# A hand-written step order for linear attention feeding a multiplicative FFN: the steps after chunk 1's first gate tile in another sequence

## The chip, the cores and the metric

The kernel runs on one core of a Trainium2 chip. The metric is the device time of one execution in microseconds (us). The kernel before takes 247.02 us as the median of three runs, which lie between 246.37 and 248.18 us.

## The reference

Eight batches of eight heads, 576 positions and 64 features per head go through a linear attention, and its output, as 4608 tokens of 512 features, goes through a feed-forward block with a product in its middle:

```
phi(x) = max(x, 0) + 1 where x > 0, exp(x) otherwise          # elu + 1
kv  = einsum('bhsd,bhde->..', phi(k), v);  z = sum_s phi(k)   # per batch and head: 64 x 64, and 64
x   = (phi(q) @ kv) / (phi(q) @ z + 1e-6)                     # 4608 tokens x 512
out = ((x @ w1) * (x @ w2)) @ w3 @ w_out                      # 512 -> 1024 -> 1024 -> 512
```

## The kernel before

**Chunks.** A batch is a chunk of 512 tokens; the 64 left over of every batch are gathered into a ninth chunk, number 8. Weights, phi, the attention products and the FFN are in bf16 with f32 sums. At the start, w3 and w_out are multiplied into one 1024 x 512 matrix wf_sb (steps E, C, w, u). Then each chunk runs through the stages below, and the stages of several chunks overlap.

**Steps.** The whole program is one string, ORDER, that `step` (L644) reads word by word. Every word issues a few instructions, each on its own engine, and every engine runs what it was given strictly in that order. So ORDER sets five queues at once: those of the TensorE (PE), VectorE (DVE), ScalarE (ACT), GpSimd (POOL) and SyncE (SP). A trailing `+` is the variable alt: a copy goes to DVE and not to ACT, a load goes on POOL's queue and not on SP's, and in step A the `+1e-6` goes to ACT and not to DVE. With b the chunk:

- L, M, N b.g load half g of k, q, v (512 KB each, L112) into one of 13 buffers of the pool `ld`; R b.0 loads the tails of q and k (four DMAs of 64 KB, L122), R b.1 those of v.
- x, X (exp on ACT, L187), y, Y (max and add on DVE, L192) and z, Z (min on DVE, L216) make phi of k and of q; part 2 is the tail. v b.i casts v (L222, tail L228).
- T b transposes phi(q) by a DMA from SP (L276). K b makes kv on PE (L252) and copies it out of PSUM (L261).
- A b.j makes 128 normalised tokens: four matmuls (L317), then an add (L334 on DVE or L332 on ACT), a reciprocal and a product on DVE (L335, L336). j = 4 is the tail. D b transposes the result into the tile xt by a DMA from SP (L361); for chunks 0 and 1 step P does it on PE (L351, L352).
- F c.f and the pair h, i are one tile of (x @ w1) * (x @ w2) for chunks 0 to 2: eight matmuls of 512 columns into two PSUM banks (L372), a copy on ACT (L377), a product on DVE (L378).
- G c.q.i is the same for chunks 3 to 8 in a Strassen-like form with seven products instead of eight: four matmuls of 256 columns (L435), then one of L464, L467, L473 on ACT, L470 and L474 on DVE; m is the closing product (L479). d c.i makes the differences of xt (L420) and e w.i those of the weights (L409) that it needs.
- O c.m multiplies by wf_sb (eight matmuls of 512 columns, L550) and copies out (L552); S and H store. Q is the last of these.

**PSUM and other limits.** F, G and the last O take four PSUM banks (`mm_ps`), G's accumulators and O two banks (`o_ps`), K and A share one double bank (`at_ps`, `bufs=1`), so A waits for the product of the A before it. Chunk c's F or G tiles need the whole tile xt, so the first of them waits for the landing of D c. SP keeps eight DMAs in flight at most: each new one waits for the eighth before it.

**Gates.** `GATES` makes two loads wait for another step's DMA (R6.0 for T3.0, M2.1 for B0.0).

Of the kernel before, what the change touches and what calls it, by code (L numbers as in the profile page):

```python
# [20 lines left out]
def kernel(  # L21
# [570 lines left out]
    E4 E3 C0 E1 E0 I0 M0.0 C1 I1+ C2 I2+ W0.8 w4 W1.5 w3+ R0.1 v0.2 Y0.0 u4.0 u3.0 C3 w1+ R0.0 E5
    w0+ E6 L0.1+ E2 u1.0 u0.0 E7 M0.1+ u4.1 u3.1 L0.0+ u0.1 x0.2 u0.2 u3.2 y0.2 u1.1 u1.2 z0.2 u3.3+
    u4.2 u4.3 u1.3 w5+ w6 N0.1 N0.0+ u0.3+ u5.0 u5.1 u6.0 u6.1 X0.0 y0.1 Z0.0 M1.1+ u6.2 x0.1 u6.3+
    z0.1 w2 Y0.1 X0.1 w7 M1.0+ R1.0+ B3.0 L1.0+ Z0.1 u5.2 y0.0 u5.3 u2.0 u2.1 x0.0 u2.2 u2.3+ B3.1
    a0.0+ z0.0 u7.0 u7.1 a0.1+ X1.1 Y1.1 u7.2 K0 N1.1 L1.1+ X1.0 I3 Z1.1 a0.2 R1.1+ Y1.0 u7.3 A0.2
    a1.1 A0.3 W2.4 A0.0 P0.2 A0.1 Z1.0 x1.2 x1.0 y1.0 P0.3 W3.2 A0.4 y1.2 N1.0 P0.0 W4.2 P0.1 y1.1
    B2.0 x1.1 v1.2 z1.2 B2.1 a1.0 z1.0 B1.0 z1.1 F0.7 F0.6 K1+ F0.4 a1.2 A1.2 F0.5 B0.0 I4 P1.2 A1.1
    B1.1 F0.2 B0.1 P1.1 M2.1 M3.1 A1.3 F0.3 P1.3 X2.1 R2.0+ A1.0 L2.1 h0 h1 Y2.1 P1.0 M2.0 h2 h3
    Z2.1 i0 i1 X3.1 R3.0+ A1.4 x2.1 F1.7 F1.6 x2.2 y2.2 Y2.0 M3.0 z2.2 e1.0 R2.1 x3.2 X2.0 Z2.0 N2.0  # L600
    y2.1 z2.1 L2.0 O0.0 Y3.0 X3.0 N2.1 R3.1 F1.0 T2.0 v2.0+ F1.3 L3.0 v2.2 L3.1 R4.0 Z3.0 O0.2 Y3.1
    x2.0 y2.0 z2.0 e1.1 y3.2 z3.2 N3.1 v2.1 F1.2 O0.1+ N3.0 S0.0 e0.2 K2 F1.5 A2.2 Z3.1 x3.0 F1.4
    A2.1+ F1.1 x3.1 A2.0+ y3.0 O0.3 T3.0 S0.1 y3.1 A2.3+ D2.0 z3.0 z3.1 v3.2 v3.0 v3.1 O1.2+ O1.3
    R4.1 e1.3 R6.0+ M4.0 M4.1 e0.0 e0.1 e0.3 K3 O1.0 A3.1+ O1.1 L4.0 A3.2+ e1.2 F2.1 A3.0+ N4.1 F2.5
    A3.3+ D3.0 Y4.0 L4.1 v4.2 F2.7 S1.1 N4.0 Y4.1 y4.2 X4.1 Z4.1 F2.2 A2.4+ x4.2 X4.0 F2.0 v4.1 z4.2
    Z4.0 T4.0 F2.3 M5.1 d3.2 L5.0 M5.0 S1.0 y6.2 L5.1 d3.0 R5.0+ F2.4 y5.2 d3.1 x6.2 x4.0 y4.0 z4.0
    G3.1.1 F2.6 A3.4+ v4.0+ y4.1 G3.1.3 x4.1 z4.1 G3.1.2 x5.2 O2.2 G3.1.4 z5.2 d3.3 G3.1.5 m3.1.5
    G3.0.4 G3.0.1 K4 z6.2 G3.0.3 G3.1.6 G3.1.7 A4.2+ G3.0.5 N5.0 y5.0 R5.1+ v5.2 m3.0.5 G3.0.2 Y5.1
    X5.1 O2.3 S2.1 G3.0.7 x5.0 Z5.1 G3.0.6 z5.0 Y5.0 A4.0+ X5.0 Z5.0 O2.1 m3.0.6 x5.1 O2.0 y5.1 L6.0
    N5.1 L6.1 G3.3.1 G3.3.4 S2.0 T5.0 A4.1+ z5.1 G3.2.1 m3.1.6 G3.3.3 G3.2.4 G3.2.3 G3.3.5 G3.3.2  # L610
    v5.0 G3.2.5 A4.3+ D4.0 G3.3.7 G3.2.2 v5.1 G3.3.6 G3.2.7 G3.2.6 m3.2.5 m3.2.6 x6.1 O3.1 x6.0 K5
    m3.3.5 M6.1 D1.1 m3.3.6 O3.3 y6.0 z6.0 y6.1 A5.2 z6.1 O3.2 d4.0 d4.1 d4.2 A5.0+ d4.3 G4.1.1
    G4.1.4 R6.1 X6.1 Y6.1 Z6.1 D3.1 O3.0 A5.1+ G4.1.3 G4.1.6 G4.0.1 G4.1.5 v6.2 G4.0.4 A5.3 G4.0.3
    G4.1.7 G4.0.2 G4.0.5 N6.0 v6.0 m4.1.5 G4.1.2 G4.3.1 G4.0.6 G4.0.7 A4.4+ G4.3.3 N7.1 G4.3.4 M6.0
    Y6.0 G4.2.1 G4.3.5 D5.0 d5.0 G4.3.6 X6.0 Z6.0 N6.1 G4.2.3 G4.2.2 G4.2.4 S3.1 G4.3.7 G4.2.5
    G5.0.4 v6.1 d5.1 m4.1.6 G4.2.6 G5.1.1 G4.2.7 m4.3.6 d5.2 K6 m4.3.5 L7.0 m4.0.5 G5.0.1 m4.2.5
    G5.1.2 L7.1 d5.3 G5.1.3 m4.0.6 G5.0.3 G5.0.6 G5.1.4 G5.0.5 G5.0.2 G5.1.5 G5.0.7 m4.2.6 G4.3.2
    T6.0 A6.3+ G5.1.7 y7.1 S3.0 x7.0 x7.1 O4.2 A6.0 R7.0 O4.1 y7.0 G5.2.1 z7.0 A6.2 z7.1 G5.1.6
    G5.3.1 N7.0 G5.3.4 G5.2.3 A6.1 G5.3.3 G5.2.2 G5.2.4 G5.3.5 x7.2 G5.2.5 G5.3.2 M7.1 G5.3.7 X7.1
    M7.0 G5.2.6 m5.0.6 G5.2.7 Y7.0 m5.2.5 R7.1 v7.2 m5.1.6 m5.1.5 m5.3.5 D6.0 d6.2 d6.0 Y7.1 A5.4+  # L620
    O4.3 S4.1 d6.1 m5.2.6 v7.1 O4.0 Z7.1 X7.0 Z7.0 y7.2 z7.2 G6.1.1 v7.0 G6.1.4 G5.3.6 O5.0 G6.1.3
    G6.3.4 T7.0 S4.0 m5.0.5 G6.1.6 d6.3 G6.0.1 D5.1 G6.1.2 A6.4+ m5.3.6 G6.1.5 G6.0.3 G6.0.4 G6.2.4
    G6.0.5 K7+ G6.1.7 G6.0.7 m6.1.6 G6.0.2 A7.1 G6.3.1 O5.2 G6.3.3 G6.0.6 G6.2.1 G6.3.5 G6.3.2 A7.4
    G6.2.3 G6.3.7 m6.0.6 G6.2.2 G6.2.6 G6.2.5 m6.2.5 O5.1 D7.1 m6.1.5 d8.0 G6.3.6 G6.2.7 d8.1 m6.3.6
    S5.0 A7.3+ O5.3 G8.0.1 G8.0.4 G8.1.1 d8.2 A7.0 G8.0.3 G8.0.6 G8.1.3 d8.3 G8.0.5 G8.1.4 G8.1.5
    S5.1 G8.2.4 G8.0.7 G8.0.2 G8.1.7 G8.1.2 m6.2.6 G8.2.1 G8.1.6 m6.0.5 G8.3.1 m6.3.5 G8.2.3 G8.2.6
    G8.3.3 m8.1.5 G8.2.5 G8.3.4 G8.3.5 G8.3.2 G8.2.7 A7.2+ G8.2.2 G8.3.7 D7.0 d7.0 m8.0.6 O6.2 O6.1
    O6.0 S6.0 O6.3 G7.0.1 d7.1 d7.3 d7.2 G8.3.6 m8.3.6 G7.1.1 S6.1 G7.0.3 G7.0.4 m8.3.5 G7.1.3
    G7.0.5 m7.0.5 G7.1.4 G7.1.5 G7.0.6 G7.0.7 G7.0.2 G7.1.7 G7.1.6 G7.2.1 G7.1.2 m8.0.5 G7.3.1
# [121 lines left out]
```

## Time and profile before

| | us |
|---|---|
| median of three runs | 247.02 (246.37 to 248.18) |
| span of the profiled execution, first to last instruction | 245.6 |
| the profiled execution's own time | not recorded beside its span; the runs are 0.8 to 2.6 above the span |
| PE busy | 230.7 |
| DVE busy | 189.6 |
| ACT busy | 158.9 |
| POOL busy | 37.8 |

The granted TensorE clock is 0.999 in this execution, so nothing is lost there. The busy time of PE contains overlaps of matmuls that follow each other: a 512-column matmul is shown with 379 ns, and eight of them in a row take 1.73 us of the chain of waits, 0.216 us each. DVE instructions overlap too: a product that is shown with 0.69 us holds its engine for 0.60 us. The 16 DMA engines are busy in nine tenths or more of the time until two thirds of the span, then little.

### The profile page before, as it was taken

The numbers are of one execution on the slowest core, as the hardware profiler recorded it, in microseconds if no ns is written. First come the engines' busy times: TensorE is split into PE (matmuls) and PEld (weight loads), VectorE is DVE, ScalarE is ACT, GpSimd is POOL, SyncE is SP. The second block draws the span as 40 slices with busy tenths as digits, with TensorE's granted clock in tenths as the row PEclk, the third lists the DMA queues.
The fourth block names the chain that finished last, engine by engine and source line by source line (L and its number), as shares of the span: only waits on it lengthen the run. The fifth ranks groups of instructions, "written<-read, shape, count | busy, mean of one in ns | idle before, by whom it ended". The sixth has DMA issues, their size and how long they took to land.

```text
span 245.6 us, 4685 instructions
## 1 busy us (share of the span) xinstructions
PE 230.7 (94%) x1713; PEld 146.7 (60%) x1713; DVE 189.6 (77%) x416; ACT 158.9 (65%) x296; POOL 37.8 (15%) x61
## 2 busy tenths in 40 slices
...
DMA  7999999999999999999999999987281320440065
GB/s 147 195 202 299 297 244 216 192 236 312 295 185 303 287 198 270 190 335 291 353 324 180 229 245 263 269 242 164 85 157 49 103 93 0 88 171 3 0 191 151
DMA packets 68343, 49.46 MB, mean 201 GB/s; under 512 B 37088, under 2 KB 63456, under 8 KB 68320
## 3 DMA queue, kind: packets, MB, share of 16 engines
...
## 4 chain that ended last, share of the span: by engine, by line
PE 69%; DMA 12%; DVE 10%; ACT 5%; issue 2%; POOL 0%; DVEq 0%; ACTq 0%; POOLq 0%
PE o_ps L550 19%; PE gu L435 15%; PE gt L435 11%; PE a_ps L372 9%; PE b_ps L372 8%; DMA w3b<-in_moe_w_dram 7%; DMA q<-in_q_dram 5%; PE nd L317 3%; DVE y L192 2%; DVE spare L470 2%; PE kvp L252 1%; DVE xn L336 1%; ACT e L187 1%; DVE kj L216 1%; DVE ab L474 1%
## 5 line engine op out<-in xcount | busy, mean ns | idle before, releaser
L550 PE MATMUL o_ps<-wf_sb,ab 128*128 128x512 bf16 x280 | 64.2, 379 | 0.0
L550 PEld LDWEIGHTS <-ab 128*128 128x128 bf16 x280 | 26.9, 98 | 29.1 <-DVE ab L474 0.8
L552 ACT COPY o_sb<-o_ps 128x512 f32<-128x512 f32 x31 | 18.1, 584 | 26.1 <-PE o_ps L550 24.9
L435 PEld LDWEIGHTS <-w_sb 128*128 128x128 bf16 x288 | 28.0, 98 | 6.8 <-issue 2.0
L372 PEld LDWEIGHTS <-w_sb 128*128 128x128 bf16 x192 | 18.2, 98 | 19.4
L372 PE MATMUL b_ps<-xt,w_sb 128*128 128x512 bf16 x96 | 25.6, 379 | 0.0
L372 PE MATMUL a_ps<-xt,w_sb 128*128 128x512 bf16 x96 | 25.6, 379 | 0.0
L336 DVE TENSOR_TENSOR xn<-nd,r 128x512 bf16<-128x512 f32 x30 | 20.7, 691 | 2.1
L378 DVE TENSOR_TENSOR ab<-a_sb,b_ps 128x512 bf16<-128x512 f32 x24 | 16.1, 683 | 6.5 <-ACT a_sb L377 3.9
L187 ACT ACTIVATE e<-q 128x1024 bf16<-128x1024 f32 x16 | 17.0, 1060 | 5.8 <-DMA q<-in_q_dram 5.7
L435 PEld LDWEIGHTS <-wt_sb 128*128 128x128 bf16 x192 | 18.2, 98 | 4.1 <-issue 0.3
L435 PEld LDWEIGHTS <-spare 128*128 128x128 bf16 x192 | 18.7, 98 | 2.2
L187 ACT ACTIVATE e<-k 128x1024 bf16<-128x1024 f32 x16 | 16.9, 1061 | 3.8 <-DMA k<-in_k_dram 3.8
L479 DVE TENSOR_TENSOR ab<-spare 128x256 bf16<-128x256 f32 x48 | 18.5, 417 | 0.1
L435 PE MATMUL gu<-spare,wt_sb 128*128 128x256 bf16 x96 | 18.3, 272 | 0.2
L435 PE MATMUL gu<-spare 128*128 128x256 bf16 x96 | 18.3, 272 | 0.0
L470 DVE TENSOR_TENSOR spare<-spare,gt 128x512 f32<-128x512 f32 x24 | 16.2, 680 | 2.2 <-PE gt L435 2.2
L470 DVE TENSOR_TENSOR spare<-spare,gu 128x512 f32<-128x512 f32 x24 | 16.2, 680 | 2.0 <-PE gu L435 1.9
L162 PE MATMUL wf_ps<-wt_sb,w3t 128*128 128x512 bf16 x64 | 15.3, 379 | 2.5 <-DMA wt_sb<-in_moe_w_out_dram 1.1
L317 PE MATMUL nd<-kv,qt 128*128 128x130 bf16 (+1 forms) x160 | 15.8, 220 | 1.5 <-ACT kv L261 1.3
L377 ACT COPY a_sb<-a_ps 128x512 f32<-128x512 f32 x24 | 13.6, 585 | 5.3 <-PE a_ps L372 5.1
L317 PEld LDWEIGHTS <-qt 128*128 128x128 bf16 (+1 forms) x160 | 11.2, 99 | 8.8 <-issue 3.3
...
## 6 DMA issues: line engine op xcount, KB each, us to landing
...
```

Source lines behind the costliest of these rows:

```text
L162: nc.tensor.matmul(wfs[i], w3ts[i][:, kc, :], wo_sb[:, kc, :], start=(kc == 0), stop=(kc == FC - 1))
L187: nc.scalar.activation(out=e, in_=x, func=AF.Exp)
L317: nc.tensor.matmul(nds[g][rows, i * 2 * E1:(i + 1) * 2 * E1], w, kvs[b % 2][:, i, g].rearrange("p u e -> p (u e)"), start=True, stop=True)
L336: nc.vector.tensor_tensor(out=dst.rearrange("p (g h) e -> p g h e", g=2), in0=v4[:, :, :, 0:D], in1=r[rows].unsqueeze(3).to_broadcast([n, ...
L372: nc.tensor.matmul(ps, w[:, kc, f * P:(f + 1) * P], xt_of(c)[:, :, kc, :], start=(kc == 0), stop=(kc == KC - 1))
L377: nc.scalar.copy(out=a_sb, in_=a_ps)
L378: nc.vector.tensor_mul(out=abs_[c][:, f, :], in0=a_sb, in1=b_ps)
L435: nc.tensor.matmul(t[:, w], l, r, start=(first and w == 0 and k == 0), stop=(k == 1), skip_group_check=True)
L470: nc.vector.tensor_tensor(out=s, in0=s, in1=t, op=ALU.add)
L479: (nc.gpsimd if alt else nc.vector).tensor_mul(out=abs_[c][:, f, r * HN:(r + 1) * HN], in0=s[:, 0], in1=s[:, 1])
L550: nc.tensor.matmul(o_ps, ab[:, f, m * P:(m + 1) * P], wf_sb[:, f, :], start=(f == 0), stop=(f == FC - 1))
L552: copy_of(alt)(out=rows_of(c, m // 2)[:, m % 2], in_=o_ps)
```

## The change

Up to step L2.1 the order is the same word for word; there the program has come to step h0, the first of the last two gate tiles of chunk 0, and PE to 54.85 us of the profile. The 530 steps that follow are the same steps in another sequence. In 34 of them the `+` is put on or taken off. No instruction is added or taken away, no shape changes, and GATES stays as it is. (The W steps only lose a number that nothing reads.)

```
     ORDER = """
...
-    B1.1 F0.2 B0.1 P1.1 M2.1 M3.1 A1.3 F0.3 P1.3 X2.1 R2.0+ A1.0 L2.1 h0 h1 Y2.1 P1.0 M2.0 h2 h3
-    Z2.1 i0 i1 X3.1 R3.0+ A1.4 x2.1 F1.7 F1.6 x2.2 y2.2 Y2.0 M3.0 z2.2 e1.0 R2.1 x3.2 X2.0 Z2.0 N2.0
...
+    P1.2 A1.1 B1.1 F0.2 B0.1 P1.1 M2.1 M3.1 A1.3 F0.3 P1.3 X2.1 R2.0+ A1.0 L2.1 N2.1 Y2.1 Z2.1 R3.0
+    h0 L3.0 x2.2 h1 M2.0 h2 P1.0+ M3.0 h3 e1.0 e1.1 i0 i1 Y3.1 y2.1 A1.4+ X3.1 N2.0 e0.2 F1.2 O0.0
...
     """
     GATES = "R6.0<T3.0 M2.1<B0.0"
```

The 34 changes of engine or queue:

- ACT to DVE: the copies of P1.0, O1.0, O1.1, O5.2, O5.3, O6.0, O6.1, O8.1, O8.2, v2.1, v2.2, v5.2, v6.2, v7.2 and K6, and the add of A2.0, A2.4, A3.0, A3.1, A4.2, A4.3 and A6.3.
- DVE to ACT: the copies of O0.1, O7.2 and v2.0, and the add of A1.4, A6.0, A6.2 and A7.4.
- POOL to SP: the tail loads R3.0, R5.0, R5.1 and R6.0. SP to POOL: the load N6.1.

**SP, around the transpose of chunk 2** (`xt<-xn` is D2.0 and then D3.0, `qt<-qj` is T3.0, `qk32r` and `v32r` are tails, q, k, v the 512 KB loads). Before:

```order
L276 DMA_TRANSPOSE qt<-qj 128x18x128
L560 DMA out_dram<-o_sb 128x1024
L361 DMA_TRANSPOSE xt<-xn 128x16x128
L122 DMA v32r<-in_v_dram 64x4x64 x2
L112 DMA q_1173<-in_q_dram 128x4x256
L112 DMA q_1175<-in_q_dram 128x4x256
L112 DMA k_1232<-in_k_dram 128x4x256
L112 DMA v_1267<-in_v_dram 128x4x256
L361 DMA_TRANSPOSE xt<-xn 128x16x128
```

Now:

```order
L276 DMA_TRANSPOSE qt<-qj 128x18x128
L560 DMA out_dram<-o_sb 128x1024
L361 DMA_TRANSPOSE xt<-xn 128x16x128
L112 DMA k_1191<-in_k_dram 128x4x256
L112 DMA q_1193<-in_q_dram 128x4x256
L112 DMA k_1228<-in_k_dram 128x4x256
L122 DMA qk32r<-in_q_dram 64x4x64 x2
L122 DMA qk32r<-in_k_dram 64x4x64 x2
L112 DMA v_1237<-in_v_dram 128x4x256
L112 DMA q_1241<-in_q_dram 128x4x256
L361 DMA_TRANSPOSE xt<-xn 128x16x128
```

Between the transposes of chunks 2 and 3 SP issued a tail of v and four big loads; now it issues five big loads and the four tail loads R5.0, which stood on POOL's queue.

**DVE, around the differences of chunk 3** (`spare<-xt` at L420 are the steps d3, which read the xt that D3.0 brings; L378 closes an F tile). Before:

```order
L212 TENSOR_TENSOR qj<-er,yr 128x512
L216 TENSOR_TENSOR qj<-e,y 128x4x256
L378 TENSOR_TENSOR ab<-a_sb,b_ps 128x512
L420 TENSOR_TENSOR spare<-xt 128x512
L192 TENSOR_SCALAR yr<-qk32r 128x512
L420 TENSOR_TENSOR spare<-xt 128x512
L378 TENSOR_TENSOR ab<-a_sb,b_ps 128x512
L192 TENSOR_SCALAR yr<-qk32r 128x512
L420 TENSOR_TENSOR spare<-xt,spare 128x512
```

Now:

```order
L378 TENSOR_TENSOR ab<-a_sb,b_ps 128x512
L192 TENSOR_SCALAR y<-q_1241 128x1024
L216 TENSOR_TENSOR kj<-e,y 128x4x256
L420 TENSOR_TENSOR spare<-xt 128x512
L378 TENSOR_TENSOR ab<-a_sb,b_ps 128x512
L420 TENSOR_TENSOR spare<-xt,spare 128x512
L216 TENSOR_TENSOR qj<-e,y 128x4x256
L378 TENSOR_TENSOR ab<-a_sb,b_ps 128x512
```

The first d3 stood behind the products of all F tiles but two; one F tile more is now behind it.

**ACT, around the load L5.1** (`e<-k` are x5.0 and x5.1; L552 copies O2.x out, L464 and L467 serve the first G tiles). Before:

```order
L187 ACTIVATE e<-k_1385 128x1024
L332 ACTIVATE r<-nd,eps 128x8
L187 ACTIVATE e<-q_1387 128x1024
L552 COPY o_sb<-o_ps 128x512
L187 ACTIVATE e<-k_1392 128x1024
L552 COPY o_sb<-o_ps 128x512
L464 COPY gt<-gu 128x512
L467 COPY spare<-gt_1674 128x512
L332 ACTIVATE r<-nd,eps 128x8
L464 COPY gt<-gu 128x512
```

Now:

```order
L187 ACTIVATE e<-k_1499 128x1024
L332 ACTIVATE r<-nd,eps 128x8
L187 ACTIVATE e<-k_1617 128x1024
L552 COPY o_sb<-o_ps 128x512 x2
L464 COPY gt<-gu 128x512 x2
L467 COPY spare<-gu 128x512
L332 ACTIVATE r<-nd,eps 128x8
L467 COPY spare<-gu 128x512
L467 COPY spare<-gt_1712 128x512
```

The exp of the last k half of chunk 5 stood between the copies of two O tiles, and now stands ahead of both.

More of the change, by code (lines that the diff above doesn't have):

```diff
@@ L591 @@
     ORDER = """
[L592 to L629, printed above, removed]
@@ L630 @@
-    m8.1.6 G7.2.3 G7.2.4 G7.3.3 m8.2.6 G7.3.4 G7.2.5 G7.2.2 G7.3.2 G7.3.5 G7.2.7 G7.3.6 G7.2.6
-    G7.3.7 O7.0 m8.2.5 O7.1+ S7.0 O8.2 H8.2 O8.3 O8.0 H8.3 m7.3.5 O8.1 m7.0.6 m7.1.6 S8.0 m7.2.5
-    m7.1.5 m7.3.6 m7.2.6 O7.2+ H7.2 Q7.3
+    E4 E3 C0 E1 E0 I0 M0.0 C1 I1+ C2 I2+ W0.8 w4 W0.5 w3+ R0.1 v0.2 Y0.0 u4.0 u3.0 C3 w1+ R0.0 E5
+    w0+ E6 L0.1+ E2 u1.0 u0.0 E7 M0.1+ u4.1 u3.1 L0.0+ u0.1 x0.2 u0.2 u3.2 y0.2 u1.1 u1.2 z0.2
+    u3.3+ u4.2 u4.3 u1.3 w5+ w6 N0.1 N0.0+ u0.3+ u5.0 u5.1 u6.0 u6.1 X0.0 y0.1 Z0.0 M1.1+ u6.2 x0.1
@@ new lines @@
+    u6.3+ z0.1 w2 Y0.1 X0.1 w7 M1.0+ R1.0+ B3.0 L1.0+ Z0.1 u5.2 y0.0 u5.3 u2.0 u2.1 x0.0 u2.2 u2.3+
+    B3.1 a0.0+ z0.0 u7.0 u7.1 a0.1+ X1.1 Y1.1 u7.2 K0 N1.1 L1.1+ X1.0 I3 Z1.1 a0.2 R1.1+ Y1.0 u7.3
+    A0.2 a1.1 A0.3 W0.4 A0.0 P0.2 A0.1 Z1.0 x1.2 x1.0 y1.0 P0.3 W0.2 A0.4 y1.2 N1.0 P0.0 W0.2 P0.1
+    y1.1 B2.0 x1.1 v1.2 z1.2 B2.1 a1.0 z1.0 B1.0 z1.1 F0.7 F0.6 K1+ F0.4 a1.2 A1.2 F0.5 B0.0 I4
+    P1.2 A1.1 B1.1 F0.2 B0.1 P1.1 M2.1 M3.1 A1.3 F0.3 P1.3 X2.1 R2.0+ A1.0 L2.1 N2.1 Y2.1 Z2.1 R3.0
+    h0 L3.0 x2.2 h1 M2.0 h2 P1.0+ M3.0 h3 e1.0 e1.1 i0 i1 Y3.1 y2.1 A1.4+ X3.1 N2.0 e0.2 F1.2 O0.0
@@ new lines @@
+    e0.0 y2.2 x2.1 z2.1 F1.0 L2.0 X2.0 e0.1 R2.1 Z3.1 F1.7 Y2.0 Z2.0 F1.1 z2.2 X3.0 F1.6 x3.0 y3.0
+    L3.1 x2.0 y2.0 v2.2+ v2.1+ z2.0 Y3.0 Z3.0 R3.1 F1.4 R4.1 v2.0 x3.1 O0.1 T2.0 y3.2 F1.5 K2 x3.2
+    O0.3 z3.0 N3.0 e1.2 y3.1 R4.0 N3.1 v3.2 v3.0 A2.2 S0.0 O0.2 z3.2 A2.0 T3.0 z3.1 F1.3 A2.1+
+    O1.1+ S0.1 v3.1 A2.3+ O1.0+ D2.0 K3 L4.0 M4.1 O1.2+ v4.2 A3.2+ O1.3 L4.1 y4.2 R5.0 N4.1 x4.2
+    M4.0 A3.1 e1.3 F2.1 A3.3+ x4.0 Y4.1 F2.2 A3.0 D3.0 N4.0 y4.1 X4.1 Z4.1 z4.2 F2.4 F2.0 x4.1 x5.2
+    A2.4 F2.5 Y4.0 M5.0 z4.1 d3.0 F2.3 S1.0 d3.1 X4.0 Z4.0 F2.6 y4.0 v4.1 v4.0+ G3.1.1 M5.1 d3.2
@@ new lines @@
+    F2.7 Y5.0 R6.0 A3.4+ X5.0 z4.0 Z5.0 G3.1.3 G3.1.2 O2.2 d3.3 G3.1.4 T4.0 e0.3 y6.2 G3.0.4 L5.0
+    S1.1 G3.1.5 G3.0.1 Y5.1 y5.2 K4 G3.1.6 z5.2 G3.0.3 G3.1.7 G3.0.2 X5.1 G3.3.4 G3.0.5 m3.1.5 x6.2
+    A4.3 m3.0.5 O2.1 Z5.1 G3.0.6 G3.0.7 x5.0 L5.1 y5.0 A4.0+ L6.1 x5.1 R5.1 m3.0.6 O2.3 L6.0 m3.1.6
+    O2.0 y5.1 A4.2 G3.3.1 G3.2.1 v5.2+ N5.1 z5.1 z5.0 G3.3.3 A4.1+ G3.2.3 G3.2.4 G3.3.5 N5.0 G3.3.2
+    G3.2.5 S2.1 G3.2.2 G3.3.7 G3.3.6 v5.1 G3.2.7 m3.2.5 G3.2.6 y6.1 T5.0 v5.0 m3.2.6 m3.3.6 x6.0
@@ new lines @@
+    S2.0 D4.0 y6.0 O3.1 K5 x6.1 m3.3.5 z6.0 M6.1 O3.3 R6.1 A5.2 z6.1 d4.0 O3.2 d4.2 L7.0 d4.1 A5.0+
+    G4.1.1 z6.2 G4.1.4 X6.1 O3.0 d4.3 Y6.1 A5.3 G4.1.3 Z6.1 M6.0 G4.0.4 G4.1.6 G4.0.1 G4.1.5 G4.1.2
+    A5.1+ G4.0.3 G4.1.7 G4.0.5 G4.0.6 X6.0 G4.3.1 m4.1.5 R7.1 v6.2+ D1.1 G4.0.7 Y6.0 G4.0.2 A4.4+
+    G4.3.3 Z6.0 G4.2.1 G4.3.4 G4.3.5 G4.2.3 G4.2.4 G4.3.6 N6.0 v6.0 D5.0 G4.2.5 M7.1 G4.2.6 G4.3.7
+    G4.2.7 d5.0 m4.1.6 N6.1+ d5.1 v6.1 m4.3.5 d5.2 G4.3.2 d5.3 G4.2.2 G5.0.1 G5.1.1 m4.0.6 T6.0
+    m4.2.6 K6+ L7.1 m4.3.6 S3.1 S3.0 G5.0.3 G5.0.4 M7.0 G5.1.3 G5.0.5 m4.0.5 G5.0.2 G5.1.4 G5.1.5
@@ new lines @@
+    G5.0.7 G5.1.2 m4.2.5 A6.0+ G5.1.7 x7.1 Y7.1 O4.2 y7.1 x7.0 D3.1 A6.1 O4.1 v7.2+ G5.0.6 A6.2+
+    G5.2.1 G5.3.1 G5.1.6 G5.2.3 A6.3 G5.3.3 z7.1 N7.0 G5.3.4 G5.2.4 G5.3.5 G5.2.5 G5.2.2 A5.4+ D6.0
+    R7.0 G5.3.7 m5.2.5 G5.3.2 G5.2.7 G5.3.6 G5.2.6 D5.1 X7.1 X7.0 Z7.1 O4.3 Y7.0 d6.0 y7.0 v7.0
+    Z7.0 O4.0 A6.4+ x7.2 G6.1.1 y7.2 d6.1 m5.2.6 z7.2 G6.1.4 d6.2 S4.1 d6.3 m5.1.5 O5.0 G6.1.2
+    G6.1.3 G6.1.6 m5.1.6 G6.0.1 G6.0.4 S4.0 N7.1 m5.0.5 G6.1.5 G6.0.3 z7.0 G6.3.4 G6.0.6 m5.3.6
+    v7.1 G6.0.5 G6.1.7 T7.0 G6.2.4 m5.0.6 K7+ G6.0.7 m6.1.5 G6.0.2 G6.3.1 m5.3.5 A7.4+ O5.2+ G6.3.3
```

9 lines of the change are left out of this document (added).

## The prediction

> **What bounds the kernel now.** I read the page first, then busy time by stage, then the chain of waits and the queues of ACT, SP and POOL. The page says that PE is the busiest engine and that the DMA engines are busy until two thirds of the span:
>
> ```profile
> PE 230.7 (94%) x1713; PEld 146.7 (60%) x1713; DVE 189.6 (77%) x416; ACT 158.9 (65%) x296; POOL 37.8 (15%) x61
> DMA  7999999999999999999999999987281320440065
> ```
>
> An average over stages doesn't tell what the change can win. Here are the stages that follow the first moved step. They are cut where PE reaches h0 (54.85), K2 (72.79), F2.1 (90.77), G3.1.1 (103.84), G4.1.1 (136.78) and G6.1.1 (174.07); the columns are length, then busy time of PE, PEld, DVE, ACT and POOL, then clock and DMA:
>
> ```profile
> 54.85:72.79 17.94, 17.94 (x91) 8.23 (x89) 15.34 (x29) 14.40 (x22) 0.00 (x0) 1.00 1.13 261
> 72.79:90.77 17.98, 17.98 (x125) 9.54 (x124) 15.50 (x30) 10.66 (x21) 4.05 (x7) 1.00 1.08 267
> 90.77:103.84 13.07, 13.07 (x69) 6.03 (x68) 10.31 (x21) 8.88 (x18) 2.06 (x4) 1.00 1.10 239
> 103.84:136.78 32.94, 31.29 (x241) 20.91 (x240) 30.55 (x66) 26.49 (x52) 0.00 (x0) 1.00 1.09 294
> 136.78:174.07 37.29, 36.93 (x313) 28.24 (x311) 35.47 (x84) 31.95 (x65) 0.00 (x0) 1.00 0.88 219
> 174.07:245.60 71.53, 68.16 (x519) 48.81 (x517) 49.43 (x114) 38.70 (x81) 0.00 (x0) 1.00 0.34 93
> ```
>
> PE is idle for 0.0 us in the first three, 1.65 in the fourth, 0.36 in the fifth; the 3.4 us of the last are nearly all the end, when the last tile is copied and stored. So 2.0 us of idle time is all that an order can win back by this view, and something less visible: matmuls are shown with overlapping ends, so a short wait makes a row longer and not idle.
>
> DVE is the second engine. It has 2.6, 2.5 and 2.8 us of idle time in the first three stages, 2.4 in the fourth, 1.8 in the fifth and 22.1 in the last. In the fourth it carries the chain:
>
> ```profile
> 119.44 0.68 DVE spare L470
> 120.12 0.60 DVE kj L216
> 120.72 0.60 DVE y L192
> 121.32 0.12 DVE r L335
> ...
> 121.54 0.69 DVE xn L336
> 122.23 0.60 DVE qj L216
> 122.83 0.35 DVE ab L479
> ...
> 123.22 0.57 ACT o_sb L552
> 123.78 0.49 ACT gt L464
> ```
>
> The starts are 0.60 us apart where a 512-column product is shown with 0.68; 0.60 is its price below, and 0.33 that of a half one.
>
> The third limit is the arrival of data. The longest idle time of PE in the fourth stage comes from a load: ACT stands 1.65 us for L5.1 (x5.1), the two copies behind it in its queue are late, and PE waits 1.03 us for a PSUM bank:
>
> ```profile
> 122.25 1.06 ACT L187 ACTIVATE e<-k 128x1024 bf16<-128x1024 f32 x1 [1.65 <-DMA k<-in_k_dram]
> 123.22 0.57 ACT L552 COPY o_sb<-o_ps 128x512 f32<-128x512 f32 x1
> ```
> ```profile
> 123.83 0.60 PE L435 MATMUL gu<-xt,w_sb 128*128 128x256 bf16 x4 [1.03 <-ACT o_sb L552]
> ```
>
> And the gate tiles of a new chunk start just when the transposed xt has landed. The chain has F2.1 at 90.82, and SP's queue has D2.0 at 83.93, with D3.0 and D4.0 behind:
>
> ```profile
> 81.93 0.26 PE nd L317 x4
> 82.19 3.45 PE o_ps L550 x16
> ...
> 88.50 0.23 PE nd L317 x4
> 88.72 1.73 PE o_ps L550 x8
> 90.45 0.37 PE nd L317 x4
> 90.82 0.97 PE a_ps L372 x4
> ```
> ```profile
> 83.93 3.41 SPq L361 DMA_TRANSPOSE xt<-xn  x1
> 96.35 5.54 SPq L361 DMA_TRANSPOSE xt<-xn  x1
> 130.03 1.86 SPq L361 DMA_TRANSPOSE xt<-xn  x1
> ```
>
> The views of this line and tile give the time from the start of the issue to the landing (min, median, max): for D2.0 alone, for all six xt, and for D4.0 (the longest) with two small ones beside it:
>
> ```profile
> DMA to landing us min/median/max: 6.8/6.8/6.8
> DMA to landing us min/median/max: 4.2/5.3/7.5
> DMA to landing us min/median/max: 3.2/5.1/6.2
> ```
>
> D2.0 lands at 83.93 + 6.8 = 90.73, and PE starts F2.1 within 0.1 us of that. D3.0, the longest with 7.5, lands at 103.85, just when G3.1.1 starts. D4.0 lands at 136.2, 0.6 ahead of G4.1.1.
>
> **The change part by part.** *No work is added.* PE's matmuls are the same, so the time changes only by what PE waits.
>
> *Copies that change engine.* Six more O copies go to DVE than leave it (6 x 0.60 = 3.6), P1.0 comes (0.6), v2.1 and v2.0 cancel, K6 comes (two of 0.43), the adds make 3 x 0.16 = 0.5. The prices:
>
> ```profile
> L552 DVE COPY o_sb<-o_ps 128x512 f32<-128x512 f32 x4 | 2.8, 688 | 7.6 <-PE o_ps L550 7.6
> L261 DVE CAST kv<-kvp 64x260 bf16<-64x260 f32 x4 | 1.7, 424 | 0.0
> L222 DVE CAST vt<-v 128x1024 bf16<-128x1024 f32 x2 | 1.4, 694 | 0.0
> L334 DVE TENSOR_SCALAR r<-nd 128x8 f32<-128x8 f32 (+1 forms) x17 | 2.7, 161 | 0.6 <-PE nd L317 0.5
> L228 ACT CAST vr<-v32r 64x256 bf16<-64x256 f32 x16 | 6.5, 405 | 2.0 <-DMA v32r<-in_v_dram 1.8
> ```
>
> The eight casts of a tail of v (v2.2, v5.2, v6.2, v7.2) were never on DVE. Bounds: 0.17 each, a quarter of L222's cast of four times the size, and 0.43, the cast of kv of the same size out of PSUM. I take 0.3, between them, as the source is SBUF like L222's: 2.4. In all DVE gets 8 us and ACT loses as much. ACT has idle time in every stage (3.5, 7.3, 4.2, 6.5, 5.3, 32.8), so its gain is worth nothing unless it stood in front of PE. Counting both orders with these prices, 2.0 us more DVE work stand ahead of G3.1.1, where DVE idles 7.8 us: covered. Between G3.1.1 and G6.1.1 it is 1.0 more, where DVE idles 4.2 but also makes PE wait; 0 to +1.0, I take **+0.3**. The other 5 fall behind G6.1.1 and are covered by 22.1.
>
> *O0.0.* Two differences of weights (e1.0, e1.1, 2 x 0.60) now stand on DVE ahead of the products i0 and i1, which were at 58.70 us; O0.0, no longer behind F1.7 and F1.6, needs both some 2 us after h3. 0 to +0.6, I take **+0.2**.
>
> *D2.0 and F2.1.* From A2.3 on PE (81.93) to the landing of D2.0 went 2.0 + 6.8 = 8.8 us, and PE filled them with A2.3 (0.26), four O tiles (4 x 1.73), K3 (1.1) and two A (0.23 and 0.37). In the new order three O tiles, K3 and two A stand behind A2.3: 1.73 less, 7.2 in all. If the landing takes as long, PE waits 1.6 us. If it goes like the fastest xt (4.2), it is there after 6.2, and the wait is 0. Against the long end speaks that the tails that POOL issued during D2.0's flight are gone from there:
>
> ```profile
> 85.80 0.62 POOL L122 DMA_DIRECT2D qk32r<-in_q_dram  x1 [32.76 <-DVE o_sb L552]
> ...
> 90.39 1.22 POOL L122 DMA_DIRECT2D qk32r<-in_k_dram  x2
> ```
>
> The row of D2.0 itself is nearer to the long end than the fastest; I take **+0.5**, a third of the way, for the empty POOL queue. The Trainium skill (DMA: Bandwidth & Descriptors, section Queues, rings and completion order) says that each DMA engine goes round between the queues that have work, one packet at a time. By that rule POOL's 256 KB of R6.0 took their share beside D2.0, 1.0 us as an estimate at the 267 GB/s of that stage's row, and D2.0 would now land so much sooner: this term would be 0 and the time 0.5 lower, 246.9. No run here shows D2.0 without them.
>
> *D3.0 and G3.1.1.* The way of PE from the A3 that releases D3.0 to G3.1.1 is the same, five F tiles and A2.4. SP has five big loads and four tails between D2.0 and D3.0, where it had four and two, but POOL's ten tails no longer fly beside them: 2.9 MB in both orders. If only SP's own queue counts, it is one load of 512 KB more, 2.2 us at that stage's 239 GB/s; if all bytes count, 0. d3.0 on DVE is now ahead of F2.3's product, so a late landing also holds a bank that F2.7 needs. I take **+0.3**.
>
> *G3.1.1 to G4.1.1.* In ACT's queue x5.1 now stands ahead of two O copies, and no longer between them and the first G copies. If L5.1 lands as early against PE's place as before, the 1.03 us wait goes with part of the other 0.6. -1.65 to 0; I take **-1.2**.
>
> *D4.0 and G4.1.1.* On SP the store S2.0 now lies between T5.0 and D4.0, 512 KB or 1.8 us at that stage's 294 GB/s, PE may come 1.2 us sooner, and there was 0.6 us to spare: 0 to +2.4. I take **+0.3**, near 0, since SP starts D4.0 only when A4.1 is done, as before. Behind it the DMA share falls to 0.34, and I take 0.
>
> Sum: 0.3 + 0.2 + 0.5 + 0.3 - 1.2 + 0.3 = **+0.4 us**. The profiled span of 245.6 becomes 246.0. The median of the runs lies 1.4 above the span, so the forecast is 247.0 + 0.4 = **247.4 us**.
>
> **The rivals.** (1) *Faster: all waits of the middle fall.* For it: every idle time of PE after 54.85 follows a late load or DVE, and the order moves these. D2.0 and D3.0 land in time, the 2.0 us are won, and the restarts that the chain shows with 0.97 where the row beside them has 0.86 give some 0.8 more: 247.0 - 2.8 = **244.2**. Against: the fullest queue, DVE, gets more work.
>
> (2) *Slower: the transposes from SP come after PE.* One mechanism at three places: an xt that lands later than PE arrives stops PE in full, since nothing else stands ahead in its queue. By the long ends above it is 1.6 at F2.1, 0.6 more at G3.1.1 (2.2 less the 1.6 that the loads have gained there) and 2.4 at G4.1.1; with the 0.5 of DVE and O0.0 and less the 1.2 won it makes +3.9: **250.9**. It decides from about 1.3 us of lateness at each of the three. For it: D2.0 and D3.0 landed within 0.1 us of PE's need, and A2.3 has one O tile less behind it. Against: the DMA engines carry no more bytes.
>
> (3) *The order does nothing of note.* It was judged over disturbed transfers, the profile has loads that land steadily, and PE's matmuls are the same: 247.0, inside the forecast's own class.
>
> **How the numbers follow.** Forecast with (3), within 1% of before (244.55 to 249.49): 0.55, own range 245.4 to 249.3. Rival (1): 0.15. Rival (2), with DVE's +1.0 and other places that I haven't priced: 0.30. A measurement here tells about 1% from no change. The range for 8 in 10 goes from 244.4, near (1), to 251.0, just beyond (2).
>
> **What would show it.** Right: PE idle before F2.1 of 0.3 to 1.0 us released by DMA xt, busy DVE up by 6 to 9 us and ACT down by as much, ACT's wait for k around 122 us gone or without a wait of PE behind it. Wrong: PE idle in the stretch from K2 to G3.1.1 above 3 us, a wait of PE on DVE of over 1 us in total between G4.1.1 and G6.1.1, or an L228 row on DVE outside 0.17 to 0.43 us.

## The result and the profile after

The changed kernel takes **250.11 us** (median of four runs, 249.3 to 250.77) where the kernel before takes 246.93 beside it. The ratio of the two sets of runs is 1.0121, with a 95% interval from 1.0083 to 1.016 (the two medians alone give 1.0129). The time is inside the range of the prediction (244.4 to 251.0), 2.7 us above its forecast of 247.4, and slower by over 1%, which had a chance of 0.30. The likeliest case, "within 1%", was wrong by the measured ratio, though the interval reaches into it.

The profiled execution took 250.65 us with a span of 248.6, so 2.0 us lie outside the span. The page's busy times and its row of DMA:

```profile
PE 231.2 (93%) x1694; PEld 146.9 (59%) x1713; DVE 197.1 (79%) x436; ACT 153.5 (62%) x276; POOL 30.1 (12%) x48
DMA  7999999999998999999999899984691120440065
```

Busy time by stage, cut where PE reaches the same steps as in the prediction (h0, K2, F2.1, G3.1.1, G4.1.1, G6.1.1, end; columns as there):

```profile
55.33:75.90 20.57, 19.72 (x97) 8.97 (x97) 19.93 (x37) 15.94 (x23) 0.00 (x0) 1.00 1.08 268
75.90:92.25 16.35, 15.93 (x115) 8.78 (x116) 12.08 (x26) 8.13 (x18) 0.00 (x0) 1.00 0.91 230
92.25:105.24 12.99, 12.99 (x71) 6.05 (x69) 11.35 (x25) 9.71 (x16) 0.00 (x0) 1.00 1.14 262
105.24:139.13 33.89, 31.63 (x239) 20.93 (x240) 31.01 (x69) 24.48 (x45) 0.00 (x0) 1.00 1.07 273
139.13:177.80 38.67, 38.08 (x316) 28.64 (x319) 37.35 (x88) 31.38 (x61) 0.76 (x1) 1.00 0.85 208
177.80:248.60 70.80, 67.04 (x507) 48.29 (x510) 52.08 (x119) 36.04 (x76) 0.00 (x0) 1.00 0.35 98
```

PE is now idle for 0.85 and 0.42 us in the first two stages, where it was 0.0, and for 2.26 in the fourth, where it was 1.65. DVE works 19.93 of the first 20.57 us.

The steps between two of these places are not the same in both orders, so lengths can't be subtracted. What PE *lost* in a stage can: its length, less what its matmuls take back to back in the same records (0.216 us with 512 columns, 0.109 with 256, 0.055 with up to 130, 0.110 with 260). For the two profiled executions, in us:

| | start of h0 | h0 to F2.1 | to K4 | to G4.1.1 | to G5.1.1 | to Q7.3 | lost in all | span |
|---|---|---|---|---|---|---|---|---|
| before | 54.85 | 0.87 | 0.81 | 2.68 | 0.63 | 2.05 | 7.04 | 245.6 |
| after | 55.33 | 1.88 | 0.91 | 3.45 | 1.46 | 1.75 | 9.45 | 248.6 |

The 3.0 us between the spans are 0.48 of a later h0, ahead of which no step changed; 2.41 of waits; and 0.1 behind Q7.3. Two places show the largest of the new waits. At F1.1, ACT stands for the load M2.0 (its exp is X2.0), and the copy that PE needs is behind it:

```profile
66.56 1.06 ACT L187 ACTIVATE e<-q 128x1024 bf16<-128x1024 f32 x1 [1.43 <-DMA q<-in_q_dram]
68.14 1.02 PE L372 MATMUL b_ps<-xt,w_sb 128*128 128x512 bf16 x4 [0.75 <-ACT a_sb L377]
```

At O2.3, ACT's copy of O2.1 needs an `o_sb` buffer. There are two, and the store S1.1, which must empty the second, was issued at 114.57 and landed at 121.21:

```profile
114.57 0.48 SPq L560 DMA_DIRECT2D out_dram<-o_sb  x1
121.29 0.58 ACT L552 COPY o_sb<-o_ps 128x512 f32<-128x512 f32 x1 [2.53 <-DMA out_dram<-o_sb]
121.93 3.61 PE L550 MATMUL o_ps<-wf_sb,ab 128*128 128x512 bf16 x16 [1.44 <-ACT o_sb L552]
```

And the wait for L5.1, which the prediction took off, is gone as such: no row of ACT waits for k there. The wait for a store stands in its place.

### The profile page after: what moved, and what is told of

The parts are those of the page before. It is cut to its first block, busy times and chain, and to the rows that moved or that the text cites. A ratio compares the mean times of both kernels' runs of the same rounds, so it can differ in the third digit from the quotient of the medians.

```text
span 248.6 us, 4659 instructions
## 1 busy us (share of the span) xinstructions
PE 231.2 (93%) x1694; PEld 146.9 (59%) x1713; DVE 197.1 (79%) x436; ACT 153.5 (62%) x276; POOL 30.1 (12%) x48
## 4 chain that ended last, share of the span: by engine, by line
PE 62%; DMA 24%; ACT 4%; DVE 4%; issue 2%; SPq 1%; POOL 0%; ACTq 0%; DVEq 0%; POOLq 0%
PE o_ps L550 19%; PE gu L435 15%; PE gt L435 10%; DMA q<-in_q_dram 9%; PE a_ps L372 6%; PE b_ps L372 6%; DMA out_dram<-o_sb 5%; DMA k<-in_k_dram 5%; DMA wt_sb<-in_moe_w_out_dram 3%; DMA xt<-xn 3%; PE nd L317 3%; PE kvp L252 1%; DVE spare L470 1%; ACT e L187 1%; DVE ab L479 1%
## 5 line engine op out<-in xcount | busy, mean ns | idle before, releaser
L550 PE MATMUL o_ps<-wf_sb,ab 128*128 128x512 bf16 x265 | 63.4, 379 | 2.2 <-ACT o_sb L552 1.4
L552 ACT COPY o_sb<-o_ps 128x512 f32<-128x512 f32 x25 | 14.6, 584 | 27.0 <-PE o_ps L550 23.5
L479 DVE TENSOR_TENSOR ab<-spare 128x256 bf16<-128x256 f32 x48 | 19.0, 417 | 0.0
L378 DVE TENSOR_TENSOR ab<-a_sb,b_ps 128x512 bf16<-128x512 f32 x24 | 16.1, 682 | 2.6 <-PE b_ps L372 1.3
L467 ACT COPY spare<-gu 128x512 f32<-128x512 f32 x24 | 14.0, 587 | 6.1 <-PE gu L435 5.9
L162 PE MATMUL wf_ps<-wt_sb,w3t 128*128 128x512 bf16 x61 | 14.8, 379 | 2.7 <-DMA wt_sb<-in_moe_w_out_dram 1.1
```

The source lines that it names most:

```text
L162: nc.tensor.matmul(wfs[i], w3ts[i][:, kc, :], wo_sb[:, kc, :], start=(kc == 0), stop=(kc == FC - 1))
L378: nc.vector.tensor_mul(out=abs_[c][:, f, :], in0=a_sb, in1=b_ps)
L467: nc.scalar.copy(out=s, in_=t)
L479: (nc.gpsimd if alt else nc.vector).tensor_mul(out=abs_[c][:, f, r * HN:(r + 1) * HN], in0=s[:, 0], in1=s[:, 1])
L550: nc.tensor.matmul(o_ps, ab[:, f, m * P:(m + 1) * P], wf_sb[:, f, :], start=(f == 0), stop=(f == FC - 1))
L552: copy_of(alt)(out=rows_of(c, m // 2)[:, m % 2], in_=o_ps)
```

## The experiments

Ratios are to the kernel before in the same set of runs (its medians there 245.8, 246.8 and 246.9), with 95% intervals.

### One wait at a time

**Three buffers for the output rows**, in the changed kernel:

```
-            o_sbs[c, r] = sm.tile([P, 2, DM], F32, tag="o_sb", name="o_sb", bufs=2)
+            o_sbs[c, r] = sm.tile([P, 2, DM], F32, tag="o_sb", name="o_sb", bufs=3)
```

> The changed kernel with three buffers for the output rows o_sb instead of two. Theory A (each stall counts in full): the copy of O1.1 no longer waits for S0.0's landing nor that of O2.1 for S1.1's, so the 0.48 us ahead of K3 and the 1.60 us ahead of O2.3 go: 250.1 - 2.1 = 248.0. Theory B (given back): PE then comes to G4.1.1 sooner, but D4.0 landed only 0.05 us ahead of G4.1.1 and stands in SP's queue behind stores and loads that land no sooner, so G4.1.1 stays near 139 us after the start and only the small rest is won: 249.5 to 250.1.

Measured: 250.09 us, ratio 1.0165 (1.0116 to 1.0215). The wait for the store is gone, and that for L5.1 is back at the next place in the same two queues:

```profile
122.19 1.06 ACT L187 ACTIVATE e<-k 128x1024 bf16<-128x1024 f32 x1 [1.72 <-DMA k<-in_k_dram]
123.77 1.08 PE L435 MATMUL gu<-xt,w_sb 128*128 128x256 bf16 x8 [0.92 <-ACT o_sb L552]
```

PE loses 1.08 us there, at G3.3.1, and another 1.08 at G4.1.1, where it was 0.26: the stage from K4 to G4.1.1 loses 3.45, as much as with two buffers. Theory B.

**O2.1 and O2.3 exchanged**, so that the second buffer is wanted later:

```
-    A4.3 m3.0.5 O2.1 Z5.1 G3.0.6 G3.0.7 x5.0 L5.1 y5.0 A4.0+ L6.1 x5.1 R5.1 m3.0.6 O2.3 L6.0 m3.1.6
+    A4.3 m3.0.5 O2.3 Z5.1 G3.0.6 G3.0.7 x5.0 L5.1 y5.0 A4.0+ L6.1 x5.1 R5.1 m3.0.6 O2.1 L6.0 m3.1.6
```

> The changed kernel with O2.1 and O2.3 exchanged, so that the first two tiles of chunk 2's output share a buffer and the second buffer (S1.1) is wanted only by the third. Theory A: the 1.60 us ahead of O2.3 goes, 248.5. Theory B (given back at G4.1.1, which waits for D4.0): 249.8 to 250.1. Theory C, the prediction's slower rival (the transposes on SP come after PE, stores have nothing to do with it): 250.1, with the stall before the third O2 tile still there.

Measured: 249.60 us, 1.0155 (1.0103 to 1.0206). The stall ahead of the third O2 tile is gone, against theory C, and of its 1.60 us 0.65 came back at G3.3.1, behind L5.1, and 0.49 at G4.1.1:

```profile
122.62 1.06 ACT L187 ACTIVATE e<-k 128x1024 bf16<-128x1024 f32 x1 [1.29 <-DMA k<-in_k_dram]
124.20 1.08 PE L435 MATMUL gu<-xt,w_sb 128*128 128x256 bf16 x8 [0.49 <-ACT o_sb L552]
```

**M2.0 ahead of R3.0 and L3.0:**

```
-    ... L2.1 N2.1 Y2.1 Z2.1 R3.0 h0 L3.0 x2.2 h1 M2.0 h2 ...
+    ... L2.1 N2.1 Y2.1 Z2.1 M2.0 R3.0 h0 L3.0 x2.2 h1 h2 ...
```

> The changed kernel with the load M2.0 ahead of R3.0 and L3.0 in SP's queue. Theory A: M2.0 lands at about 64 us instead of 66.5, the exp X2.0 no longer holds up ACT's copy of F1.1's first product, and the 0.91 us of PE at F1.1 goes: 249.2. Theory B (what is won is given back at the next late landing): 250.1, with L3.0 or S0.0 taking the wait.

Measured: 249.40 us, 1.0141 (1.0087 to 1.0195). The exp X2.0 has its load in time (first row here) and nothing is lost at F1.1; 0.90 is lost at A2.0 instead, 12 us later, where DVE's queue is late with the product of A2.2 (second row). In this execution PE also lost 0.91 and 0.76 at G4.3.7 and G4.2.7 (third row, the first of the two), where the changed kernel loses 0.27.

```profile
64.05 1.07 ACT L187 ACTIVATE e<-q 128x1024 bf16<-128x1024 f32 x1
...
79.75 0.40 PE L317 MATMUL nd<-kv,qt 128*128 128x130 bf16 x4 [0.74 <-DVE xn L336]
...
152.09 0.60 PE L435 MATMUL gu<-spare,w_sb 128*128 128x256 bf16 x4 [0.74 <-DVE spare L470]
```

That this is the edit's doing isn't shown. The kernels with O2.1 and O2.3 exchanged (above) and with e0.3 moved (next) have the changed kernel's steps word for word up to there, with M2.0 where it was. In their profiles, too, nothing is lost at F1.1 or K3, and 0.90 and 0.89 at A2.0, as in this row of the first:

```profile
80.49 0.40 PE L317 MATMUL nd<-kv,qt 128*128 128x130 bf16 x4 [0.73 <-DVE xn L336]
```

M2.0 landed at 65.2 and 64.9 us in these two and at 66.5 in the changed kernel's profile. Up to F2.1 the three lost 1.44, 1.41 and 1.88 us. So the place of a wait of this size differs between executions of the same steps, and one profile doesn't tell what an edit did to it.

**e0.3 moved on DVE** to where it idles:

```
-    F2.7 Y5.0 R6.0 A3.4+ X5.0 z4.0 Z5.0 G3.1.3 G3.1.2 O2.2 d3.3 G3.1.4 T4.0 e0.3 y6.2 G3.0.4 L5.0
+    F2.7 Y5.0 R6.0 A3.4+ X5.0 z4.0 Z5.0 G3.1.3 G3.1.2 O2.2 d3.3 G3.1.4 T4.0 y6.2 G3.0.4 L5.0
     (and "e0.3" ahead of O1.2+)
```

> The changed kernel with the weight difference e0.3 moved on DVE from behind T4.0 to just ahead of O1.2's copy, where DVE idles 2.5 us. Theory A: the 0.49 us of PE ahead of G3.1.6 goes, 249.6. Theory B: O2.3 waits for S1.1's landing at 121.2 us all the same, so what is won here is lost there: 250.1.

Measured: 249.40 us, 1.0132 (1.0086 to 1.0178). The 0.49 us ahead of G3.1.6 is gone, 0.55 stands ahead of G3.1.7, and O2.3 waits for S1.1 as in the changed kernel, with 1.64 us lost:

```profile
120.29 0.58 ACT L552 COPY o_sb<-o_ps 128x512 f32<-128x512 f32 x1 [2.57 <-DMA out_dram<-o_sb]
120.92 1.24 PE L550 MATMUL o_ps<-wf_sb,ab 128*128 128x512 bf16 x5 [1.48 <-ACT o_sb L552]
```

**e0.0, e0.1 and e0.3 there**, out of the stage in which DVE is full:

```
-    ... O0.0 e0.0 y2.2 x2.1 z2.1 F1.0 L2.0 X2.0 e0.1 R2.1 ... O1.2+ ... T4.0 e0.3 y6.2
+    ... O0.0 y2.2 x2.1 z2.1 F1.0 L2.0 X2.0 R2.1 ... e0.0 e0.1 e0.3 O1.2+ ... T4.0 y6.2
```

> The changed kernel with the weight differences e0.0 and e0.1 taken out of the stage in which DVE is full (55 to 80 us, 24 of 25 us busy) and put, with e0.3, just ahead of O1.2's copy, where DVE idles 2.5 us; there the kernel before has them. Theory Q (DVE's queue from 55 to 80 us): the 0.9 us ahead of A2.0 and the 0.49 ahead of G3.1.6 go, 248.9. Theory B: given back between K4 and G4.1.1, where the loads set the pace: 249.5 to 250.

Measured: 249.35 us, 1.0112 (1.007 to 1.0155). PE loses 0.63 us from h0 to F2.1, less than before the change, but h0 itself began at 56.08 in this execution, so everything that it needs had 0.75 us more to arrive. K4 to G4.1.1 loses 3.03.

None of the five differs from the changed kernel by more than the intervals, which reach 1.0 to 1.3 us to each side: a gain of less than 1 us could not be seen. In the three made for O2.3 or G3.1.6 the wait is gone from its place, and most of it or all stands at later places of the same profile. For F1.1 and A2.0 the profiles don't separate the edit from what another execution or a later start does.

### The same wait in the order before

The -1.2 us of the prediction can be tried without the rest: in the kernel before, only x5.1 moves in ACT's queue.

```
-    X5.1 O2.3 S2.1 G3.0.7 x5.0 Z5.1 G3.0.6 z5.0 Y5.0 A4.0+ X5.0 Z5.0 O2.1 m3.0.6 x5.1 O2.0 y5.1 L6.0
-    N5.1 L6.1 G3.3.1 G3.3.4 S2.0 T5.0 A4.1+ z5.1 G3.2.1 ...
+    X5.1 O2.3 S2.1 G3.0.7 x5.0 Z5.1 G3.0.6 z5.0 Y5.0 A4.0+ X5.0 Z5.0 O2.1 m3.0.6 O2.0 y5.1 L6.0
+    N5.1 L6.1 G3.3.1 G3.3.4 x5.1 S2.0 T5.0 A4.1+ z5.1 G3.2.1 ...
```

> The kernel before with one step moved: x5.1 in ACT's queue from between the copies of O2.1 and O2.0 to behind those of G3.3.1 and G3.3.4. This is the -1.2 us of the prediction alone, without relying on when L5.1 lands. Theory W (that stall counts in full): the 1.03 to 1.2 us of PE ahead of G3.2.1 go and the time falls by 1.0 to 1.6 us. Theory B: D4.0 was only 0.6 us ahead of G4.1.1, so 0.5 us at most.

Measured: 246.64 us, 1.0011 (0.998 to 1.0042): no change. The wait ahead of G3.2.1 is gone, and 1.03 us is lost three products later, at G3.2.3. There ACT has no idle time in front of it; it does the exp first, then an add, then the copy for which PE waits:

```profile
122.67 1.06 ACT L187 ACTIVATE e<-k 128x1024 bf16<-128x1024 f32 x1
123.62 0.27 ACT L332 ACTIVATE r<-nd,eps 128x8 f32<-128x8 f32 x1
123.77 0.61 ACT L464 COPY gt<-gu 128x512 f32<-128x512 f32 x1
...
124.43 0.38 PE L435 MATMUL gu<-spare,wt_sb 128*128 128x256 bf16 x2 [0.86 <-ACT gt L464]
```

L5.1 had landed at 120.5 here, 1.7 us sooner than in the profile of before, so this time it wasn't the load: an exp of 1.06 us among copies that PE waits for cost about its own length in both places. In this profile the stage from K4 to G4.1.1 lost 2.00 us where the profile of before lost 2.68, but twelve runs show no gain, and by their interval it is 0.5 us at most.

### The order and the engines apart

The new sequence with all 34 engines and queues of before:

```
-    ... A1.0 L2.1 N2.1 Y2.1 Z2.1 R3.0 h0 L3.0 x2.2 h1 M2.0 h2 P1.0+ ...
+    ... A1.0 L2.1 N2.1 Y2.1 Z2.1 R3.0+ h0 L3.0 x2.2 h1 M2.0 h2 P1.0 ...
     (and the other 32 likewise)
```

> The new sequence of steps with every copy and load on the engine and queue of before: the order alone. Theory S (SP's stream of loads is what PE waits for, and the 14 tail loads moved onto it made it longer): the tails fly beside SP's transposes again, D4.0 lands by 1.5 us or more earlier against the start of chunk 0's last gate tiles, and most of the loss goes: 247.5 to 248.5. Theory D (DVE's 8 us of extra work): the same sum, but with D4.0 as late as now. Theory O (the sequence itself): 250.

The changed kernel with only the five load steps back (R3.0+, R5.0+, R5.1+, R6.0+, N6.1):

> The changed kernel with only the five load steps back on their queues (R3.0, R5.0, R5.1, R6.0 on POOL's, N6.1 on SP's); copies and adds as changed. Theory S: D4.0 lands earlier by 1.5 us or more and the time is 247.5 to 248.5. Theories D and O: 250, with D4.0's landing as now.

The kernel before with only these five changed (R3.0, R5.0, R5.1, R6.0, N6.1+):

> The kernel before with only the five load steps on the queues of the change (R3.0, R5.0, R5.1, R6.0 on SP's, N6.1 on POOL's). Theory S: D4.0 lands 1.5 us later or more and the time rises by 1.5 to 3 us over before. Theories D and O: no change.

The kernel before with only the 29 copies and adds changed:

> The kernel before with only the 29 copies and adds on the engines of the change (8 us more work on DVE, 8 less on ACT). Theory D: 1 to 3 us slower than before. Theories S and O: within 0.5 us of before, as the prediction had it with +0.3 for DVE.

| order | loads | copies and adds | us | ratio |
|---|---|---|---|---|
| before | before | new | 254.67 | 1.0339 (1.0284 to 1.0395) |
| before | new | before | 263.66 | 1.0655 (1.0604 to 1.0705) |
| new | before | before | 252.47 | 1.0226 (1.0184 to 1.0267) |
| new | before | new | 249.95 | 1.0147 (1.0089 to 1.0205) |
| new | new | new | 250.11 | 1.0121 (1.0083 to 1.016) |

Every theory missed something. The order alone is slower than the whole change: it is the sequence of steps that costs, and the changes of engine take a part of it back. The 29 copies gain 0.8% in the new order (the two intervals overlap by 0.2%) and cost 3.4% in the old one, half of it at the end: of the 15.0 us that PE loses there, 7.3 lie behind G6.1.1, where the kernel before loses 0.9, and PE waits for DVE, which now copies O6.0, O8.1 and others between its products:

```profile
217.70 0.59 PE L550 MATMUL o_ps<-wf_sb,ab 128*128 128x512 bf16 x2 [1.22 <-DVE o_sb L552]
243.90 0.73 PE L550 MATMUL o_ps<-wf_sb,ab 128*128 128x512 bf16 x2 [1.17 <-DVE ab L479]
```

The five loads cost nothing that can be seen in the new order (these two rows come from different sets of runs) and 6.5% in the old one, where R5.0 stands in the written order just behind L5.1 and ahead of its use. On POOL's empty queue it was issued at 89.2, 22 us ahead of L5.1; on SP it is issued behind L5.1, at 110.8, and lands at 121.0:

```profile
121.12 0.43 DVE L192 TENSOR_SCALAR yr<-qk32r 128x512 bf16<-128x512 f32 x1 [17.04 <-DMA qk32r<-in_k_dram]
121.94 0.61 PE L435 MATMUL gu<-spare,wt_sb 128*128 128x256 bf16 x2 [16.16 <-DVE spare L420]
```

A part of the loss comes behind that wait: in this profile the granted clock was 0.50 from 109.9 us to 127.0, and until then PE's matmuls of 512 columns followed each other at 0.43 us and not 0.216, which is some 2 us more.

With the loads back in the new order, D4.0 landed at 136.23 and not 139.08 (h0 came 0.84 earlier), as theory S had it, and the stage from K4 to G4.1.1 lost 1.40 instead of 3.45. But two things took its place: 2.47 instead of 1.88 up to F2.1, and at K6 a wait for N6.1, which the change had put on POOL's queue:

```profile
154.64 1.05 ACT L222 CAST vt<-v 128x1024 bf16<-128x1024 f32 x1 [2.05 <-DMA v<-in_v_dram]
155.74 0.39 PE L252 MATMUL kvp<-vt,kj 128*128 128x130 bf16 x4 [1.39 <-ACT vt L222]
```

So the last part of it was tried with N6.1 left on POOL's queue and only the tails back (R3.0+, R5.0+, R5.1+, R6.0+):

> The changed kernel with R3.0, R5.0, R5.1 and R6.0 back on POOL's queue, and N6.1 left on POOL's, where the change put it. With N6.1 back on SP as well, D4.0 came 2.8 us sooner and PE then lost 1.6 us more at K6, which waits for N6.1. Theory S: the stage from K4 to G4.1.1 loses 1.4 us instead of 3.45 and K6 loses nothing new: 248.4 to 249. Theory B (what is won is given back at a late landing behind it): 250.

Measured: 248.89 us, 1.0102 (1.006 to 1.0143). K6 waits no more, K4 to G4.1.1 loses 1.39, and h0 to F2.1 now 3.48, 1.01 of it at A2.0 and 1.71 at F2.1. The latter is the transpose D2.0: R6.0 is gated by T3.0, and on POOL's queue it starts 0.8 us behind D2.0. The view of D2.0, first in the changed kernel, then with the tails on POOL's queue (who waited for it, and the landing):

```profile
DMA to landing us min/median/max: 4.5/4.5/4.5
```
```profile
  PE a_ps L372: 1.6, 1
DMA to landing us min/median/max: 6.8/6.8/6.8
```

And three edits together: the tails back, e0.0, e0.1 and e0.3 late, and

```
-    ... A4.0+ L6.1 x5.1 R5.1 m3.0.6 O2.3 L6.0 m3.1.6 O2.0 y5.1 A4.2 G3.3.1 G3.2.1 v5.2+ ...
+    ... A4.0+ L6.1 R5.1+ m3.0.6 O2.3 L6.0 m3.1.6 O2.0 y5.1 A4.2 G3.3.1 G3.2.1 x5.1 v5.2+ ...
```

> The changed kernel with the four tails back on POOL's queue, e0.0, e0.1 and e0.3 as in the run beside it, and the exp x5.1 moved in ACT's queue from ahead of the copies of O2.3 and O2.0 to behind G3.2.1's. If the waits add up: 0.9 at A2.0, 2.0 from K4 to G4.1.1 and 0.5 at G3.1.6, so 246.5 to 247.5, level with before. If the sequence has other costs: 249.

Measured: 251.53 us, 1.0207 (1.0162 to 1.0252), worse than the first two alone (248.89 and 249.35; x5.1 wasn't moved alone in the new order). D2.0 took 6.6 us again (1.53 lost at F2.1); 0.79 was lost at K3 and 0.66 at A2.2, and h0 began at 57.08: PE's first wait for a piece of w3, in code that no edit touches, was 2.8 us in this execution and 0.2 in the changed kernel's. Why that start came late isn't settled.

No kernel was faster than the one before. One with R6.0 alone on SP and the other tails on POOL, which both rows of D2.0 and of K4 point to, wasn't tried.

## Why the prediction came out as it did

- **The -1.2 us from G3.1.1 to G4.1.1 is the step that failed.** It rested on "if L5.1 lands as early against PE's place as before". L5.1 landed at 123.32, 1.1 later, PE stood 1.60 us for S1.1 instead, and the stage from K4 lost 0.77 more, not less. Even alone, in the old order, the edit won nothing that the runs show. The prediction took one wait off and didn't ask what is late next: S1.1, L5.1 and D4.0 each stopped PE in one of the profiles above where another was out of the way.
- **h0 to F2.1:** forecast +0.2 at O0.0 and +0.5 at F2.1, measured +1.01, with 0.0 at both places. It is 0.91 at F1.1, behind M2.0, and 0.48 at K3, where O1.1's copy, now on DVE, waits 1.02 us for the store S0.0 with A2.3's product queued behind it. The waits for stores were in no term and no rival. This is the split of one execution; the two others with the same steps lost 0.54 and 0.57 more than before, nearly all at A2.0, behind DVE.
- **D2.0:** I took a third of the long end, since POOL's tails no longer fly beside it. From issue to landing D2.0 took 4.3 to 4.6 us in the seven profiles that have R6.0 on SP's queue, in either order, and 5.3 to 6.8 in the seven that have it on POOL's. The Trainium skill (DMA: Bandwidth & Descriptors, section Queues, rings and completion order) has each DMA engine go round between the queues that have work; by that rule the term was 0, and it was 0. The rule's estimate of 1.0 us is short of the measured difference (6.8 against 4.5); how the engines shared their time, the runs don't show.
- **D3.0 and D4.0:** D3.0 landed 0.4 us ahead of G3.1.1 (forecast +0.3, measured 0). D4.0 landed 0.05 ahead of G4.1.1, which lost 0.26 (forecast +0.3).
- **DVE +0.3:** DVE is up by 7.5 us and L228 costs 0.29 on it, as forecast (8; 0.3). But ACT fell by 5.4, not by as much. G4.1.1 to G5.1.1 lost 0.83 more, and 1.80 against 1.46 with all 34 engines and queues back, so it is the order of the products there and not the engine (in the old order the new engines of the 29 cost 0.33 there).
- **DVE ahead of G3.1.1, priced at nothing:** the prediction called 2.0 us more work there covered by 7.8 us of idle time, which it had added up over three stages. The work came in the first. From 55 to 80 us DVE was busy for 21.89 us before and 24.14 after (third figure of the rows), and the waits at A2.0 in six of the profiles above are for DVE:

```profile
55.00:80.00 25.00, 25.00 (x143) 12.05 (x141) 21.89 (x43) 18.39 (x30) 0.00 (x0) 1.00 1.11 274
55.00:80.00 25.00, 24.15 (x138) 11.90 (x138) 24.14 (x46) 18.48 (x29) 0.00 (x0) 1.00 1.02 257
```

- **The base:** I took the time to be 1.4 above the span, from a median and a profile of different executions. Where both are known of the same run, it is 1.7 to 1.8 for the kernel before and 2.0 to 2.1 for the changed one (250.65 less 248.6); every kernel here with the four tails on SP's queue lies at 2.0 to 2.1, every one with them on POOL's at 1.7 to 1.9. So about 0.25 us of the loss lies outside the span, and the profile of before, with 245.6, was some 0.4 slower than the median.

Rival (2) gave 250.9 and the time came close, but not by its mechanism: in the changed kernel's profile no transpose came after PE by more than 0.3 us (with the tails on POOL's queue D2.0 did: PE lost 1.40 at F2.1 in the order alone, 1.71 and 1.53 in the two runs above). Waits for a store and for loads on the same queue, and waits for DVE, came in place of that, and the experiments don't split the loss between them. So it is luck that the time lies inside the range, whose upper end was that rival's. Of the signs of being right, DVE's 7.5 us came; the wait for L5.1 was gone, but with a wait of PE for a store in its place; and PE's idle time before F2.1 did not come.
